# One Strassen chain over all 512 tokens of a block, with the activation sums made by accumulating DMAs

## The chip, the cores and the metric

The kernel runs on one core of a Trainium2 chip. The metric is the device time of one execution in microseconds (us). The kernel before takes 364.61 us (median of three runs, 363.89 to 365.18).

## What is computed

```python
scores = scale * q @ k.T + bias[head, i - j]          # 8 batches, 8 heads, 576 tokens, 64 channels
x = softmax(scores) @ v                               # as 4608 tokens x 512
h = x @ w_in                                          # 512 x 2048
g = h + sin(alpha * h) ** 2 / (alpha + 1e-9)
out = g @ w_out                                       # 2048 x 512
```

## The kernel before, in words

The work is cut in eight **stages**, one for each batch (attention over 576 tokens), and nine **blocks** of 512 tokens for the two products behind it. Stage t does the attention of batch t, then the *input product* of block t: 16 slices f of 128 of the 2048 inner channels, each four matmuls of 512 columns on TensorE (`pb<-xT,w_in`), a sine on ScalarE (L1132), a square on ScalarE or VectorE (L1139, L1141), and on VectorE the sum that gives slice f of `g` (L1146). The *output product* `g @ w_out` of block t runs during the attention of stage t+1, in the places where TensorE would wait for ScalarE. All matmuls are issued by the helper `full` (L500).

In the attention of a stage, runs of three score products (`pb<-qT,kT`) go into three pairs of PSUM banks, ScalarE takes the exponential of each (L749, 128x1024), VectorE multiplies the bias in (L780), TensorE multiplies with the values (`pb<-v,u` and `pb<-vh,u`), VectorE divides (L999, L1000), and the result is turned into `xT` by DMA transposes on SP's queue (L1079, L970) or by TensorE (L1088) with a copy (L581 on ScalarE, L583 on VectorE).

**The output product before.** Of each block's four groups of 128 tokens, two are done plainly (`plan_mo`: 16 matmuls of 512 columns each). The other two are done together by one Strassen-Winograd chain (`plan_chain`): seven products of eight matmuls of 256 columns in place of eight, with combinations of `w_out` made once (`wsum`) and four sums of quarters of `g` made for each block on VectorE (L1364, in four pieces each, into the tile `ss` or in place in `g`). The products are added up on VectorE out of PSUM (`take`, L1421), half a row block at a time, and each 128 tokens are stored (L1409). Blocks 0, 7 and 8 are done otherwise and stay so.

**The order of the work** is set ahead of time by a planner inside the kernel: every piece of work is a task with an estimated duration, dependences and a priority, and `Plan.run` writes the tasks down engine by engine. Each engine then runs its instructions strictly in that order; a wait holds up all that stands behind it on that engine. GpSimd (POOL) and SP issue the DMAs and are such engines too.

**GpSimd's queue before**, in each stage: the copies `kt<-kT` (L445), which wait for the transposed keys of the next batch; a one-element copy (`tick`, L1172) that waits for the first slice of `g`; four loads of values (L450) and two of their tails (L469) for the next batch; and the staging of keys and queries of the batch after that in half precision (L433, DRAM to DRAM).

**SP's queue before**, in each stage: the DMA transposes of `xT`, the stores, and the transposes of the staged keys and queries (L439, L440).

Of the kernel before, what the change touches and what calls it, by code (L numbers as in the profile page):

```python
# [35 lines left out]
NBUF = {"ut": 2, "ss": 1, "u": 2, "g": 2, "s16": 3, "sq": 3, "outs": 5, "xn": 6}  # L36
# [28 lines left out]
class Plan:  # L65


    def __init__(self):
        self.tasks = []
        self.sin = self.in_qk = False  # L70
# [26 lines left out]
    def pick(self, b, taken):  # L97
        sets = PAIRS if b.tag == "sc" else ((6, 7),) if b.tag == "av2" else [(k,) for k in BANKS[b.tag]]
        best = None
# [56 lines left out]
    def run(self, t0):  # L156
        free = {e: t0 for e in ("PE", "ACT", "DVE", "POOL", "SP")}
        todo = list(self.tasks)
        while todo:
            best = None  # L160
            cands = {e: [] for e in free}
# [64 lines left out]
QUOTA = 47  # L226
QUOTA1 = 28
OFFSET = 0
# [20 lines left out]
LATE = 100  # L249
# [8 lines left out]
AV_AT = (3, 4, 6, 7)  # L258
AV_D = (0, 0, 300, 0)
AV_G = (3, 7)  # L260
PRE = -100
# [3 lines left out]
MOEP = (5, 25)  # L265
STEP = 700
MIX = "nnssss"
# [3 lines left out]
MIX0 = "nnssss"  # L271
FIRST = 1
CH = ("mo", "mo", "mo", "st")
PIECES = 4
AV_LATE = 9900
AV0 = 1500
FILL_GAP = 0.05
# [11 lines left out]
AV_PRI = 0  # L289
NORM_PRI = 200  # L290
# [17 lines left out]
def kernel(  # L308
# [78 lines left out]
    xv = zz  # L387
# [13 lines left out]
    def new_g():  # L401
        return tp.tile([128, NF, DM], F16, name="g", tag="g", bufs=2)
# [16 lines left out]
    def new_ss():  # L419
        return tp.tile([128, 6, 512], F16, name="ss", tag="ss", bufs=NBUF["ss"])  # L420

    def new_outs():
        return tp.tile([128, DM], F32, name="outs", tag="outs", bufs=NBUF["outs"])
# [425 lines left out]
    def plan_att(t, gates, gate):  # L849
# [10 lines left out]
        for i, units in enumerate(runs):  # L860
# [20 lines left out]
            def run(e, i=i, made=made, tl=tl, fresh=fresh):  # L881
# [6 lines left out]
                if i == len(runs) - 1:  # L888
                    plan.in_qk = False
# [13 lines left out]
            head = [m]  # L903
            exps += [x[3] for x in made]
# [10 lines left out]
    def plan_late(base, gate):  # L915
# [12 lines left out]
        tail_alone(0, base + 1200)  # L928
        return [x[3] for x in made]

    def tail_alone(t, base):
        tl = plan_tail(t, base)
        m = plan.add({"PE": D_TAIL + 0.1}, tl[0], tl[1], base, new=[tl[2]], use=[tl[3]])
        m.marks = [(tl[4], D_TAIL)]

# [172 lines left out]
    def plan_moe_in(b, tbl):  # L1108
# [5 lines left out]
        for f in range(NF):  # L1114
# [3 lines left out]
            def mm(e, js, f=f, h=h, hb=hb):  # L1118
                if js[0] == 0:
                    h.v = bank(hb)  # L1120
# [22 lines left out]
            def gg(e, f=f, h=h, sq=sq):  # L1143
                if f == 0:
                    gcell[b].v = new_g()
                nc.vector.scalar_tensor_tensor(  # L1146
                    out=gcell[b].v[:, f, :], in0=sq.v, scalar=inv_a[:, f : f + 1], in1=h.v,
# [21 lines left out]
            if f == 0 and 1 <= b < T - 1:  # L1169

                def issue(e):
                    nc.gpsimd.tensor_copy(out=tick, in_=gcell[b].v[0:1, 0, 0:1])  # L1172
                    load_v16(b + 1)

                x = plan.add({"POOL": 6.0}, issue, [gdone[(b, 0)]] + kq_in[-1:], PB + 9500, use=[gbuf[b]])
                staged.append(x)
                if b + 2 < T:
                    to_stage.append((b + 2, x))
# [3 lines left out]
    mo_last, kq_in, staged, to_stage = [], [], [], []  # L1182

    def plan_mo(b, a, cut=NF):

        mb, ob, m = Buf("mo"), Buf("outs"), Cell()
        for f in range(NF):
# [3 lines left out]
            def mm(e, f=f):  # L1191
                if f == 0:
                    m.v = bank(mb)
                full(m.v, gcell[b].v[:, f, 128 * a : 128 * a + 128], w_out16[:, f, :], f == 0, f == NF - 1)
# [43 lines left out]
    def plan_half(b, a):  # L1238
# [10 lines left out]
        def act(i, j):  # L1249
            return gcell[b].v[:, H2 * j : H2 * j + H2, 128 * (a + i) : 128 * (a + i) + 128]  # L1250
# [90 lines left out]
    def plan_chain(b, a):  # L1341

        H2, n = NF // 2, DM // 2
        sv, sb = Cell(), Buf("ss")
        bk = [Buf(x) for x in CH]
        bv = [Cell() for _ in range(4)]
        o = Cell(), Cell()
        ob = Buf("outs"), Buf("outs")
        gall = [gdone[(b, f)] for f in range(NF)]
        base = 500000000 + 4 * b + a  # L1350

        def act(i, j):
            return gcell[b].v[:, H2 * j : H2 * j + H2, 128 * (a + i) : 128 * (a + i) + 128]

        def pre(out, x, y, op, deps, first=False):

            made = []
            for h in range(PIECES):
                r = slice(H2 // PIECES * h, H2 // PIECES * (h + 1))

                def sm(e, h=h, r=r):
# [199 lines left out]
```

## Time and profile before

| | before |
|---|---|
| median of three runs | 364.61 us (363.89 to 365.18) |
| profiled execution, first to last instruction | 361.6 us |
| busy: TensorE / ScalarE / VectorE / GpSimd | 356.0 / 316.3 / 306.1 / 93.2 us |
| granted TensorE clock | 1.000 |
| one stage (187.7 to 226.6 us): length; ScalarE, VectorE busy | 38.9; 36.57, 33.79 us |

The profiled execution has no time of its own beside its span, which is 3.0 us less than the median of the runs. In rows of the profile, `pb<-xT,w_in` reads "written: pb, read: xT and w_in"; `SPq` and `POOLq` are the issuing side of the DMA queues; "x" is a count; durations of merged rows run from the first start to the last end, and matmuls overlap, so the time from one to the next is read from starts.

### The profile page before, as it was taken

What the parts mean: (1) busy time and instruction counts of PE and PEld (TensorE: products, weight loads), DVE (VectorE), ACT (ScalarE), POOL (GpSimd) and SP (SyncE); (2) the same over time, 40 slices, a digit from 0 to 9 for tenths busy, and PEclk for the clock granted to TensorE, in tenths of its full rate; (3) what the DMA queues carried; (4) which work ended last, traced back from release to release, by engine and by line L of the source; (5) the groups of instructions that cost most, each with busy time, mean ns of one, the idle gap of its engine ahead of it and who ended that gap; (6) DMA issues with size and microseconds to landing.
All of it is one profiled execution on the core that took longest, in us unless ns stands there. A gap on an engine that the chain in (4) does not pass through costs nothing.

```text
span 361.6 us, 9613 instructions
## 1 busy us (share of the span) xinstructions
PE 356.0 (98%) x3811; PEld 218.4 (60%) x3811; DVE 306.1 (85%) x749; ACT 316.3 (87%) x436; POOL 93.2 (26%) x135
## 2 busy tenths in 40 slices
PE   8999999999999999999999999999999999999996
PEld 4564445644575447884684458545787467456685
DVE  4887888989977998699978997899869986999982
ACT  2998999999998999899989999899989998996811
POOL 8577450064000820055001900091006000000000
PEclk9999999999999999999999999999999999999999
DMA  9999999789724994299918992699339322001023
GB/s 167 206 200 188 207 160 134 142 83 124 120 48 104 138 150 101 55 158 143 137 34 159 110 169 55 127 136 143 87 81 158 66 57 54 15 3 59 31 76 101
DMA packets 150157, 40.53 MB, mean 112 GB/s; under 512 B 137224, under 2 KB 145504, under 8 KB 150112
## 3 DMA queue, kind: packets, MB, share of 16 engines
q0 software_dynamic: 96064, 17.67, 60.7%
q1 hardware_dynamic: 53872, 22.16, 26.1%
q8 instruction: 30, 0.49, 0.6%
q10 hardware_dynamic: 176, 0.09, 0.1%
q14 instruction: 15, 0.12, 0.1%
HBM read 37.73 MB, written 16.56 MB: 150 GB/s over the span
## 4 chain that ended last, share of the span: by engine, by line
PE 94%; DMA 2%; ACT 1%; DVE 1%; SPq 0%; issue 0%; DVEq 0%
PE pb L500 93%; DMA mhr<-e_dram 1%; ACT u L749 1%; DMA e_dram<-e_sb 1%; PE pb L600 1%; PE pb L1088 1%; DVE u L780 1%; DVE s L1057 0%; SPq L523 0%; ACT e_sb L649 0%; PE pb L594 0%; ACT xT L581 0%; SPq L516 0%; DVE outs L1314 0%; DVE zz L551 0%
## 5 line engine op out<-in xcount | busy, mean ns | idle before, releaser
L749 ACT ACTIVATE u<-pb 128x1024 f16<-128x1024 f32 (+1 forms) x146 | 136.8, 1020 | 6.2 <-PE pb L500 4.9
L500 PE MATMUL pb<-xT,w_in 128*128 128x512 f16 (+4 forms) x704 | 128.6, 340 | 0.3 <-ACT xT L581 0.3
L1146 DVE SCALAR_TENSOR_TENSOR g<-sq,inv_a,pb 128x512 f16<-128x512 f16 x144 | 101.4, 744 | 3.8 <-ACT sq L1139 1.8
L1132 ACT ACTIVATE s<-pb,alphaT 128x512 f16<-128x512 f32 x144 | 92.9, 693 | 12.4 <-PE pb L500 11.6
L500 PEld LDWEIGHTS <-w_in 128*128 128x128 f16 x704 | 64.5, 98 | 56.0 <-issue 0.8
L500 PE MATMUL pb<-w_out,g 128*128 128x512 f16 (+1 forms) x416 | 83.5, 339 | 0.0
L500 PEld LDWEIGHTS <-g 128*128 128x128 f16 x552 | 50.8, 98 | 34.8 <-issue 5.2
L780 DVE TENSOR_TENSOR u<-u,m2r 128x512 f16<-128x512 f16 (+1 forms) x128 | 61.5, 488 | 9.9 <-ACT u L749 9.2
L500 PEld LDWEIGHTS <-u 128*128 128x128 f16 x1280 | 55.9, 97 | 9.6 <-issue 4.9
L1139 ACT ACTIVATE sq<-s 128x512 f16<-128x512 f16 x76 | 47.5, 640 | 2.0 <-DVE g L1146 1.1
L445 POOL COPY kt<-kT 64x256 f16<-64x256 f16 x12 | 5.2, 430 | 168.0 <-DMA kT<-staged_k 167.7
L500 PE MATMUL pb<-v,u 128*128 128x65 f16 x1024 | 43.8, 193 | 0.0
L500 PE MATMUL pb<-qT,kT 64*128 64x64 f16 (+1 forms) x512 | 42.1, 285 | 0.8 <-DVE qT L583 0.3
L1141 DVE TENSOR_TENSOR sq<-s 128x512 f16<-128x512 f16 x68 | 28.4, 427 | 11.3 <-ACT s L1132 10.4
L500 PEld LDWEIGHTS <-kT 64*128 64x128 f16 x512 | 17.2, 94 | 20.5 <-issue 13.1
L500 PE MATMUL pb<-vh,u 128*128 128x130 f16 x128 | 28.3, 221 | 0.2 <-DVE s L1057 0.2
L1000 DVE TENSOR_TENSOR xn<-pb,rd 128x384 f16<-128x384 f32 (+2 forms) x53 | 26.0, 490 | 1.8
L450 POOL DMA_DIRECT2D v<-in_v_dram x28 | 24.7, 895 | 3.1 <-DMA nat<-in_k_dram 1.8
L1459 ACT ACT_TABLE_LOAD x15 | 19.2, 1283 | 0.3
L749 ACT ACTIVATE nat<-pb 128x1024 f16<-128x1024 f32 (+1 forms) x24 | 18.8, 820 | 0.0
L999 DVE RECIPROCAL rd<-pb 128x6 f32<-128x6 f32 (+2 forms) x53 | 9.9, 187 | 8.2 <-PE pb L500 7.0
L500 PE MATMUL pb<-wsum,g 128*128 128x256 f16 (+1 forms) x136 | 16.7, 267 | 0.0
(100 smaller groups left out, 311.7 us busy)
## 6 DMA issues: line engine op xcount, KB each, us to landing
out_dram<-outs SPq DMA_DIRECT2D x28, 256.0 KB, 3.0
v<-in_v_dram POOLq DMA_DIRECT2D x28, 128.0 KB, 4.8
staged_k<-in_k_dram POOLq DMA_DIRECT2D x6, 576.0 KB, 8.6
staged_q<-in_q_dram POOLq DMA_DIRECT2D x6, 576.0 KB, 12.1
w_in<-in_moe_w_in_dram POOLq DMA_DIRECT2D x4, 512.0 KB, 9.1
w_out<-in_moe_w_out_dram POOLq DMA_DIRECT2D x4, 512.0 KB, 13.5
out_dram<-outs SPq DMA_DIRECT2D x16, 128.0 KB, 1.7
w_out<-in_v_dram SPq DMA_DIRECT2D x6, 128.0 KB, 5.1
```

The costliest lines, as they stand in the source:

```text
L445: nc.gpsimd.tensor_copy(out=kts[t % 2][r, :, r], in_=kTs[t % 2][r, :, 512:S])
L450: nc.gpsimd.dma_start(out=vs[t % 2][:, c, :, 0:D], in_=vp[128 * c : 128 * c + 128],)
L500: nc.tensor.matmul(out=out, lhsT=lhsT, rhs=rhs, start=start, stop=stop, skip_group_check=go_on)
L749: nc.scalar.activation(out=o, in_=x, func=AF.Exp, scale=0.125)
L780: nc.vector.tensor_tensor(out=io, in0=io, in1=m2[:, 2 * p : 2 * p + 2, x0 : x0 + hi - lo], op=ALU.mult)
L999: nc.vector.reciprocal(out=r, in_=x[:, :, :, D])
L1000: nc.vector.tensor_tensor(out=xn[:, 0:n].rearrange("p c (z d) -> p c z d", z=2), in0=x[:, :, :, 0:D], in1=r.unsqueeze(3).to_broadcast([128 ...
L1132: nc.scalar.activation(out=s16.v, in_=h.v, func=AF.Sin, scale=alphaT[:, f : f + 1])
L1139: nc.scalar.activation(out=sq.v, in_=s16.v, func=AF.Square)
L1141: k_of(e).tensor_tensor(out=sq.v, in0=s16.v, in1=s16.v, op=ALU.mult)
L1146: nc.vector.scalar_tensor_tensor(out=gcell[b].v[:, f, :], in0=sq.v, scalar=inv_a[:, f : f + 1], in1=h.v, op0=ALU.mult, op1=ALU.add,)
L1459: nc.scalar.preload_act_table_set(name)
```

## The change

Blocks 1 to 6 lose the two plain groups. One chain now does all 512 tokens: seven products of sixteen matmuls of 256 columns. Its sums are no longer made on VectorE. Signs are turned so that only additions are needed, and each sum is a DMA of 512 KB inside SBUF that adds into its target (`accum_op`), issued by GpSimd; two plain copies on SP's queue start two of the sums. `g` is stored in another order, so that each operand of a sum is one run of 4 KB in a partition. The takes are 128x512 in place of 128x256, and a store is 512 KB. The value loads no longer stand behind the first slice of `g`; the planner puts them into the attention of the stage (with `tick` gone from there), and the staging behind the last sum and the value loads. The planner may use any free bank for the output product for a part of the stage (`roomy`), and a dozen of its numbers are others, as `QUOTA` (how much output product goes into the attention), `STEP` and `MOEP`.

```diff
-NBUF = {"ut": 2, "ss": 1, "u": 2, "g": 2, "s16": 3, "sq": 3, "outs": 5, "xn": 6}
+NBUF = {"ut": 2, "ss": 1, "u": 2, "g": 2, "s16": 3, "sq": 3, "outs": 4, "xn": 6}
...
-QUOTA = 47
+QUOTA = 41
...
+V_RUN = 4
+D_ISSUE = 1.0
+D_LAND = 4.5
+D_COPY = 1.1
...
-        return tp.tile([128, NF, DM], F16, name="g", tag="g", bufs=2)
+        return tp.tile([128, 2, 4, NF // 2, 128], F16, name="g", tag="g", bufs=2)
...
                 nc.vector.scalar_tensor_tensor(
-                    out=gcell[b].v[:, f, :], in0=sq.v, scalar=inv_a[:, f : f + 1], in1=h.v,
+                    out=gcell[b].v[:, f // 8, :, f % 8], in0=sq.v.rearrange(four, a=4),
+                    scalar=inv_a[:, f : f + 1], in1=h.v.rearrange(four, a=4),
...
-            if f == 0 and 1 <= b < T - 1:
-
-                def issue(e):
-                    nc.gpsimd.tensor_copy(out=tick, in_=gcell[b].v[0:1, 0, 0:1])
-                    load_v16(b + 1)
...
-    def plan_chain(b, a):
+    def plan_chain(b):
...
+        def act(i, j):
+            return gcell[b].v[:, j, 2 * i : 2 * i + 2]
+
+        def move(to, x, deps, add=True, new=False):
+
+            def go(e):
+                if new:
+                    s2v.v = new_ss()
+                (nc.gpsimd if add else nc.sync).dma_start(
+                    out=to().rearrange("p s f t -> p (s f t)"), in_=x().rearrange("p s f t -> p (s f t)"),
+                    **({"accum_op": ALU.add} if add else {}))
...
+            for f in range(2 * H2):
+
+                def mm(e, f=f):
+                    if f == 0:
+                        bv[k].v = bank(bk[k])
+                    s = f // H2
+                    full(bv[k].v[:, n * s : n * s + n], x()[:, s, f % H2], w()[:, f % H2], f % H2 == 0,
+                         f % H2 == H2 - 1)
...
-        s1 = pre(lambda: sums(0), lambda: act(1, 0), lambda: act(1, 1), ALU.add, gall, True)
-        s2 = pre(lambda: sums(1), lambda: sums(0), lambda: act(0, 0), ALU.subtract, [s1])
-        s3 = pre(lambda: act(1, 0), lambda: act(0, 0), lambda: act(1, 0), ALU.subtract, [s1])
-        s4 = pre(lambda: sums(2), lambda: act(0, 1), lambda: sums(1), ALU.subtract, [s2])
...
+        c2 = move(lambda: sums(0), lambda: act(1, 0), gh[0], False, True)
+        c3 = move(lambda: sums(1), lambda: act(1, 0), gh[0], False)
+        c3.go.after = [c2.go]
+        a2 = move(lambda: sums(0), lambda: act(0, 0), [c2])
+        s3 = move(lambda: sums(1), lambda: act(0, 0), [c3])
+        s2 = move(lambda: sums(0), lambda: act(1, 1), gh[1] + [a2])
+        s1 = move(lambda: act(1, 0), lambda: act(1, 1), gh[1] + [c3, c2])
+        p = prod(0, lambda: act(0, 0), wq(0, 0), gh[0])
+        x = take(0, (1, 0), None, [p], new=True)
+        p = m2 = prod(1, lambda: act(0, 1), wq(1, 0), gh[1])
+        c11 = take(1, (0, 0), (1, 0), [p, x], ALU.add, new=True)
+        s4 = move(lambda: act(0, 1), lambda: sums(0), [s2, m2])
+        p = prod(2, lambda: sums(0), ws(1), [s2] + wdone)
...
+        p = prod(3, lambda: sums(1), ws(2), [s3])
+        p = prod(5, lambda: act(1, 0), ws(0), [s1])
+        p = prod(4, lambda: act(1, 1), ws(3), [])
+        p = prod(6, lambda: act(0, 1), wq(1, 1), [s4])
...
+            if t < T - 1:
+                x = plan.add({"POOL": 5.0}, lambda e, t=t: load_v16(t + 1), [heads[V_RUN]] + heads[len(RUNS.split()):],
+                             PB + 9300)
```

`gh[0]` and `gh[1]` are the first and the last eight slices of `g`; a sum waits for its copies and sums by name, so **s2 waits for a2, which waits for the copy c2**.

**GpSimd, from one batch's `kt` copies to the next one's**, before:

```order
L445 COPY kt_70<-kT_66 64x4x64 x2
L1172 COPY tick<-g 1x1
L450 DMA v_72<-in_v_dram 128x8x64 x4
L469 DMA vh_74<-in_v_dram 64x4x64 x2
L433 DMA staged_k<-in_k_dram 4608x1x64
L433 DMA staged_q<-in_q_dram 4608x1x64
L445 COPY kt_71<-kT_67 64x4x64 x2
```

and now, where `ss<-g` and `g<-g` and `g<-ss` are the five adding DMAs a2, s3, s1, s2 and s4:

```order
L455 COPY kt_70<-kT_66 64x4x64 x2
L1366 DMA ss<-g 128x2048 x2
L1366 DMA g<-g 128x2048
L1366 DMA ss<-g 128x2048
L1366 DMA g<-ss 128x2048
L460 DMA v_73<-in_v_dram 128x8x64 x4
L479 DMA vh_75<-in_v_dram 64x4x64 x2
L443 DMA staged_k<-in_k_dram 4608x1x64
L443 DMA staged_q<-in_q_dram 4608x1x64
L455 COPY kt_71<-kT_67 64x4x64 x2
```

The value loads and the staging moved behind all five sums of the block; before, they were the first thing behind the `kt` copies.

**TensorE in block 3, at the first product that reads a sum.** Before (third product of the chain, in the later attention):

```order
L500 MATMUL pb<-v_72,u 128x65
L500 LDWEIGHTS ss
L500 MATMUL pb<-wsum,ss 128x256 [waits DVE_49]
L500 LDWEIGHTS ss
L500 MATMUL pb<-wsum,ss 128x256
```

and now (product 2, whose weights are sum s2):

```order
L510 MATMUL pb<-w_out_79,g 128x256
L510 LDWEIGHTS g
L510 MATMUL pb<-w_out_79,g 128x256
L510 LDWEIGHTS ss [waits DMASW1_49]
L510 MATMUL pb<-wsum,ss 128x256 [waits DVE_49]
L510 LDWEIGHTS ss
L510 MATMUL pb<-wsum,ss 128x256
```

The wait for VectorE's sums became a wait for a DMA of GpSimd's queue, and it stands directly behind product 1, with nothing between that could cover it.

**VectorE behind the input product of a block**, before:

```order
L1364 TENSOR_TENSOR ss<-g 128x256 x4
L999 RECIPROCAL rd<-pb 128x4
L1000 TENSOR_TENSOR xn<-pb,rd 128x256
L780 TENSOR_TENSOR u<-u,m2r 128x2x256
L780 TENSOR_TENSOR u<-u,m2r 128x2x384
L583 COPY outs<-pb 128x512
L780 TENSOR_TENSOR u<-u,m2r 128x2x384
L1364 TENSOR_TENSOR ss<-ss,g 128x256
L766 TENSOR_TENSOR u<-u,mhr 128x2x128
L1364 TENSOR_TENSOR ss<-ss,g 128x256
```

and now:

```order
L1422 TENSOR_TENSOR outs<-pb,outs 128x2x256
L790 TENSOR_TENSOR u<-u,m2r 128x2x256
L1011 RECIPROCAL rd<-pb 128x4
L1012 TENSOR_TENSOR xn<-pb,rd 128x256
L790 TENSOR_TENSOR u<-u,m2r 128x2x384
L593 COPY outs<-pb 128x2x256
L790 TENSOR_TENSOR u<-u,m2r 128x2x384
L776 TENSOR_TENSOR u<-u,mhr 128x2x128
```

The sums are gone from between the bias products, and the takes that stay are twice as wide.

More of the change, by code (lines that the diff above doesn't have):

```diff
@@ L98, in pick @@
         sets = PAIRS if b.tag == "sc" else ((6, 7),) if b.tag == "av2" else [(k,) for k in BANKS[b.tag]]
+        if b.tag == "mo" and self.roomy:
+            if all(self.bank_free(k) is None or self.bank_free(k) > self.now for k in (6, 7)):
+                sets = [(k,) for k in range(8)]
         best = None
@@ L160, in run @@
             best = None
+            self.now = free["PE"]
             cands = {e: [] for e in free}
@@ L1405, in ws, with put, take @@
             return lambda: wsum[:, k]
-        def store(i):
-            r = 512 * b + 128 * (a + i)
-            nc.sync.dma_start(out=out[r : r + 128, :], in_=o[i].v)
-        def take(k, to, x, deps, new=False, last=False):
+        def put(i, j):
+            return o[i].v[:, :, n * j : n * j + n]
+        def take(k, to, x, deps, op=None, swap=False, new=False, last=False):
             i, j = to
```

176 lines of the change are left out of this document (77 added, 99 removed).

## Prediction

> **What bounds the kernel now.** I read the page first, then the chain that ended last, then one stage by windows.
>
> ```profile
> PE 356.0 (98%) x3811; PEld 218.4 (60%) x3811; DVE 306.1 (85%) x749; ACT 316.3 (87%) x436; POOL 93.2 (26%) x135
> ...
> PE 94%; DMA 2%; ACT 1%; DVE 1%; SPq 0%; issue 0%; DVEq 0%
> ```
>
> TensorE is busy 356.0 of 361.6 us and is 94% of the chain. The chain in order of time shows how its stages follow each other (start, length):
>
> ```profile
> 148.83 38.83 PE pb L500 x468
> 187.66 0.17 PE pb L1088 x3
> 187.83 38.73 PE pb L500 x403
> 226.55 0.17 PE pb L1088 x3
> ```
>
> No other engine stands between stages of 38.9 us. But a busy TensorE may wait inside its rows, so I set ScalarE beside it in one stage's windows: input product, turn to the attention, attention.
>
> ```profile
> 188.60:202.40 13.80, 13.80 (x66) 6.26 (x64) 12.07 (x24) 12.30 (x21) 5.04 (x8) 1.00 0.79 126
> 202.40:205.00 2.60, 2.60 (x15) 1.10 (x15) 2.60 (x5) 2.58 (x5) 2.60 (x3) 1.00 2.16 146
> 205.00:227.50 22.50, 22.50 (x333) 15.41 (x333) 19.12 (x59) 21.69 (x24) 2.83 (x2) 1.00 1.10 109
> ```
>
> The columns are length, then TensorE, weight loads, VectorE, ScalarE and GpSimd busy, granted clock, DMA share and GB/s. In the 22.5 us of attention ScalarE is busy 21.69, VectorE 19.12. So TensorE bounds the stage, with ScalarE 0.8 us behind it; VectorE has 3 us to spare. What is taken from TensorE counts until ScalarE has closed up.
>
> **What the change takes from TensorE.** The times of one matmul are read from starts in the timeline.
>
> ```profile
> 188.59 13.98 PE L500 MATMUL pb<-xT,w_in 128*128 128x512 f16 x64
> 202.40 0.27 PE L500 MATMUL pb<-w_out,ss 128*128 128x256 f16 x1
> ...
> 204.98 0.82 PE L500 MATMUL pb<-qT,kT 64*128 64x512 f16 x6
> 205.73 0.25 PE L500 MATMUL pb<-vh,nat 128*64 128x130 f16 x2
> ...
> 347.93 2.78 PE L500 MATMUL pb<-wsum,u 128*128 128x256 f16 x24
> 350.55 1.04 PE L500 MATMUL pb<-w_out,u 128*128 128x256 f16 x8
> ```
>
> 64 matmuls of 512 columns take 202.40 - 188.59 = 13.81 us, 0.2158 each; 24 of 256 take 2.62, 0.1092 each. A block's output product was 32 x 0.2158 + 56 x 0.1092 = 13.02 us and becomes 112 x 0.1092 = 12.23: **0.79 us less, 4.7 us in six blocks**.
>
> Where it goes matters. Between input product and first score run stood 1 matmul of 256 and 11 of 512 columns (23 halves), now 28 halves: 0.5 us more there; the attention has 13 halves, 1.4 us, less. ScalarE is busy 21.69 us in that attention, of which one copy into `xT` (0.49 us, first row) goes to VectorE in these stages. The other rows are its waits in this one stage, in all, how often, the longest:
>
> ```profile
> 226.84 0.49 ACT L581 ACTIVATE xT<-pb 128x384 f16<-128x384 f16 x1
> ...
> ACT s L1132 <- PE pb L500: 1.5, 2, 1.2
> ACT u L749 <- PE pb L500: 0.4, 2, 0.2
> ```
>
> With 21.2 of work and the waits of 0.2 us still before a score run, the attention can't be shorter than some 21.4 us. Then the stage is 13.8 + 3.15 + 21.4 = 38.35, 0.55 us less than now, and by TensorE alone 0.79. **I take 0.6 us a block, 3.6 in all**: at such a balance the second engine keeps part, and both ends stay in the range.
>
> **VectorE.** The sums go and the takes grow:
>
> ```profile
> L1421 DVE TENSOR_TENSOR outs<-pb,outs 128x256 f32<-128x256 f32 x30 | 12.6, 420 | 1.4 <-PE pb L500 1.2
> L583 DVE COPY outs<-pb 128x512 f32<-128x512 f32 x16 | 11.0, 689 | 0.6 <-PE pb L500 0.3
> L1364 DVE TENSOR_TENSOR ss<-ss,g 128x256 f16<-128x256 f16 x24 | 6.9, 287 | 0.0
> ```
>
> Sixteen pieces of 0.29 us are 4.6 us a block; seven takes and copies of 0.42 and two copies of 0.69 were 4.3 and become eight of 0.69, 5.5. VectorE loses 3.4 us a block, none of it on the path, since TensorE hides it: I cost it at nothing. A take can now hold a bias product back 0.27 us longer; three score pairs in flight cover that, without them it is 0.27 us for each.
>
> **The new wait.** Call the start of an input product M (188.59 here). TensorE reaches product 2 in block 3 after the input product (13.8), 55 halves (6.0), two score runs and the tail of the attention before (0.75 each, from the starts 204.98 and 205.73), and one pair of 512 columns (0.43): M + 22.5. What must have landed by then is c2, a2, s2, one after the other. The slices of `g` on VectorE set their start:
>
> ```profile
> 198.08 2.05 DVE L1146 SCALAR_TENSOR_TENSOR g<-sq,inv_a,pb 128x512 f16<-128x512 f16 x3
> ...
> 203.21 2.10 DVE L1146 SCALAR_TENSOR_TENSOR g<-sq,inv_a,pb 128x512 f16<-128x512 f16 x3
> ```
>
> The first row holds slices 7 to 9 (counted from 0), the second ends with 15: eight slices are there at M + 10.2, all at M + 16.7. No trace row shows an adding DMA, nor one of 512 KB inside SBUF. The nearest is a store of 256 KB in whole rows, in a window of 0.0725 us columns:
>
> ```profile
> GB/s 0 0 0 0 0 0 0 0 0 0 0 0 282 367 424 424 395 367 282 424 367 226 57 0 18 95 201 219 201 124 42 4 0 0 1 0 0 0 0 0
> ...
> out_dram<-outs SPq DMA_DIRECT2D x1, 256.0 KB, 2.0
> ```
>
> It lands 2.0 us after its issue and moves for 0.7 us, near 380 GB/s. A copy of 512 KB is then 2.7 us. GpSimd takes longer to issue than SP (shortest, median and longest in ns):
>
> ```profile
> L450 POOL DMA_DIRECT2D v<-in_v_dram x28: 873/893/907, 33.4 to 276.9; - x28
> ...
> L1409 SPq DMA_DIRECT2D out_dram<-outs x12: 336/337/338, 110.9 to 325.5; - x12
> ```
>
> For a sum I put the lower end at 3.3 (a copy and those 0.55 us), and the upper end, for one alone, at 4.6 (every byte moved twice); below a copy it can't be, since it moves the same bytes. I take 3.9, between them. c2 lands at M + 13.0, a2 at 17.0, s2 is issued behind s1 at 17.7 and lands at 21.6: **0.9 us before it is needed, cost nothing**. That cover is thin, and each further us of a sum counts twice.
>
> **What moved on GpSimd and SP.** The value loads and the staging, before and in the rows of the page:
>
> ```profile
> 198.60 3.54 POOL L450 DMA_DIRECT2D v<-in_v_dram  x4
> 202.10 1.29 POOL L469 DMA_DIRECT2D vh<-in_v_dram  x2
> 203.34 2.28 POOL L433 DMA_DIRECT2D staged_k<-in_k_dram  x1
> 205.04 2.80 POOL L433 DMA_DIRECT2D staged_q<-in_q_dram  x1
> ...
> 229.56 2.57 SPq L439 DMA_TRANSPOSE kT<-staged_k  x1
> 232.22 2.68 SPq L440 DMA_TRANSPOSE qT<-staged_q  x1
> ...
> staged_q<-in_q_dram POOLq DMA_DIRECT2D x6, 576.0 KB, 12.1
> ```
>
> Staged queries land at 205.04 + 12.1 = 217.1 and are fetched at 232.22: 15 us of slack. Now they stand behind s4, which needs product 1 (M + 22.5): values from 23.4, queries issued at 29.8 (6.4 us on, as 198.60 to 205.04), landed at M + 41.9, against a fetch 4.7 us into the next input product, 38.3 + 4.7 = 43.0. **1.1 us of slack is left of 15**: it costs nothing while s4 is on time. Behind the waiting transpose on SP stand c2 and c3, due 5.5 us later, so only a delay of over 3 us goes round into the next block's sums. The `xT` transposes of the attention now meet the staging. The tail's pair (207 to 210 us, first row) already does, and lands in 6.6 us where the median of all `xT` transposes (second row) is 2.8:
>
> ```profile
> DMA to landing us min/median/max: 6.4/6.6/6.7
> ...
> DMA to landing us min/median/max: 2.3/2.8/6.7
> ```
>
> Between the value products whose transpose is needed last and the next input product stand, in the new order, 29 halves (3.2 us), one score run of 0.83 and five value products of 0.30:
>
> ```profile
> 222.24 0.90 PE L500 MATMUL pb<-qT,kT 64*128 64x512 f16 x34
> 223.07 1.27 PE L500 MATMUL pb<-wsum,g 128*128 128x256 f16 x10
> ...
> 224.39 0.22 PE L500 MATMUL pb<-vh,u 128*128 128x130 f16 x1
> ...
> 224.69 0.22 PE L500 MATMUL pb<-vh,u 128*128 128x130 f16 x1
> ```
>
> That is 5.5 us, less 0.8 for the division on VectorE: cost nothing at 2.8, at 6.6 up to 1.9 us a block; I keep nothing, since that pair is the slowest shown. Four output buffers for five: the previous block's last store is issued near M + 17, lands by 20, is needed at 22.5. No cost.
>
> **Sum.** 361.6 - 3.6 = 358.0 for the span; with the 3.0 us between span and median of the runs, **361.0 us**.
>
> **Rivals.**
> *TensorE alone sets the stage*: all 4.7 us, perhaps a little more where ScalarE waited: 357.5 to 359.3. For it: ScalarE has 0.8 us; against it: all of that would have to vanish.
> *ScalarE holds most of it, or small waits at product 2*: 362.6 to 365. For it: 21.69 of 22.5.
> *The sums come late (the slower side).* Place: product 2, with the next score runs and so ScalarE behind it. a2, s3, s1 and s2 share GpSimd's queue. If each byte is moved twice, each needs 4 x 0.65 = 2.6 us of all engines; four from M + 13.9 end at 24.3, and s2 lands at about 25.0, 2.5 us late. Less the 0.79 gained that is 1.7 us a block, 10 in all: 375. It decides from a landing at M + 23.3. For it: a sum has two sources; against it: four overlap only if s1, which waits for all of `g`, falls in with s2.
> *The staging comes late*: s4 over 3 us late sends the delay round, 1 us a block and more, 365 to 370.
> *GpSimd is held up by VectorE.* The value loads stand beside a VectorE 87% busy (12.07 of 13.80 us), and their issues are 873 to 907 ns each. One that waited out an L1146 instruction (some 0.7 us, three in 2.05) would spread them; a2 and s2 each that late are 1.5 us, 0.6 past the cover. The kernel would then stand at 361.0 + 3.6 = 364.6, and I give it 0.02. The Trainium skill, "SBUF — State Buffer", section "SBUF: two separate sides", says that a VectorE instruction in a two-port mode locks GpSimd out so that it can't write the descriptors of its DMAs. By that rule this is the rival that bites; the trace disagrees so far, at 873 to 907 ns.
>
> The skill's "DMA: Bandwidth & Descriptors", section "Anatomy of one DMA", puts a DMA at about 2.0 us plus its bytes at 436 GB/s. An estimate from that page for 256 KB is 2.6 us, where the store row has 2.0; for a sum of 512 KB with each byte twice it is 4.4, and s2 would land at M + 22.6, the sum unchanged to 0.1 us.
>
> **Chances.** Forecast (359.3 to 362.6) 0.48; TensorE alone 0.10; ScalarE or small waits 0.14; sums late 0.21; staging late 0.05; GpSimd held 0.02. A measurement of this kernel tells about 0.3% from no change, 1.1 us. Faster: 0.48 + 0.10 + 0.04 of the third = 0.62. Within 0.3% (363.5 to 365.7): 0.10 of the third, the 0.02, and 0.01 of the late cases, 0.13. Slower: 0.25. For 8 in 10 the range leaves out 0.05 below 358.5 and 0.13 of the late cases above 368.
>
> **What would show it.** Right: stages near 38.3 us, no wait of TensorE for a DMA of `ss`, sums landing in 3.3 to 4.6 us, ScalarE's waits below 0.2 us in the attention. Sums late: a gap of TensorE before product 2 or score rows spread there, landings over 5 us. Staging late: SP's transposes of `qT` later than 5 us into the input product. ScalarE: no gap, but exponentials end to end. Wrong altogether would be a stage of 38.9 with none of these.

## The result, and the profile after

The changed kernel takes 429.06 us (median of 4 runs, 422.76 to 429.58) against 364.62 us (363.89 to 365.18). The ratio is **1.168, 95% interval 1.159 to 1.177**: slower by a sixth, where 361.0 us was forecast and 368.0 was the range's end. Two of the four runs, 429.19 and 429.58 us, count as slow ones, so the ratio is that of the other two, 422.76 and 428.94 us. The profiled run took 428.94 us, with a span of 426.9 us and a mean granted clock of 0.943.

The page after, in the order in which it was read before: busy time of the engines; the largest group of matmuls that waits now and did not before; queue 0 (software, 60.7% before); and the issues with their median landing.

```profile
PE 367.2 (86%) x3955; PEld 236.2 (55%) x3955; DVE 295.9 (69%) x649; ACT 311.6 (73%) x428; POOL 118.3 (28%) x159
...
q0 software_dynamic: 100384, 33.40, 81.0%
...
L510 PE MATMUL pb<-wsum,ss 128*128 128x256 f16 x192 | 31.1, 314 | 42.6 <-DMA ss<-g 42.6
...
ss<-g POOLq DMA_DIRECT2D x18, 512.0 KB, 6.9
ss<-g SPq DMA_DIRECT2D x12, 512.0 KB, 3.6
out_dram<-outs SPq DMA_DIRECT2D x12, 512.0 KB, 7.2
...
g<-g POOLq DMA_DIRECT2D x6, 512.0 KB, 10.6
```

TensorE was busy 356.0 of 361.6 us, idle for 5.6. It is now busy 367.2 of 426.9, idle for 59.7. So the 65.3 us of span are 54.1 us of idle time and 11.2 us of longer busy time. Of the idle time 42.6 us are waits for DMAs into `ss`, where products 2 and 3 read their sums. The waits, in all, how often, and the longest (the first row is from the kernel before):

```profile
ACT u L749 <- PE pb L500: 4.9, 17, 1.0
...
ACT u L759 <- PE pb L510: 61.8, 27, 9.4
...
PE pb L510 <- DMA ss<-g: 42.6, 6, 8.3
...
DVE outs L1422 <- DMA out_dram<-outs: 18.4, 5, 5.7
```

Six waits, one in each block, 7.1 us each. The score runs that stand behind product 2 on TensorE start after it, and ScalarE waits with them (61.8 us, 4.9 before). One stage by windows shows it; input product, turn, attention, columns as before.

```profile
166.86:182.37 15.51, 14.13 (x130) 11.53 (x128) 12.43 (x25) 12.33 (x21) 1.59 (x3) 1.00 1.18 181
182.37:185.53 3.16, 3.16 (x31) 2.64 (x29) 3.16 (x6) 3.14 (x5) 0.99 (x2) 1.00 0.89 165
185.53:217.14 31.61, 23.89 (x340) 17.09 (x340) 16.17 (x40) 20.47 (x23) 11.83 (x11) 0.84 1.46 158
```

The input product has 1.4 us of waits for `xT`, the turn is as forecast, and the attention takes 31.6 us in place of 22.5. In that attention the timeline (start, length, engine, what; idle time before it in brackets) has GpSimd's adds first, then SP's issues, then TensorE:

```profile
181.57 0.91 POOL L1366 DMA_DIRECT2D ss<-g  x1 [6.12 <-DVE g L1161]
182.88 0.87 POOL L1366 DMA_DIRECT2D ss<-g  x1 [0.40 <-issue]
185.68 0.84 POOL L1366 DMA_DIRECT2D g<-g  x1 [1.93 <-DVE g L1161]
186.76 0.85 POOL L1366 DMA_DIRECT2D ss<-g  x1 [0.23 <-issue]
199.19 0.85 POOL L1366 DMA_DIRECT2D g<-ss  x1 [11.59 <-issue]
...
178.06 1.13 SPq L1366 DMA_DIRECT2D ss<-g  x2
184.10 2.29 SPq L1425 DMA_DIRECT2D out_dram<-outs  x2
188.04 6.17 SPq L982 DMA_TRANSPOSE xT<-xn  x2
...
190.13 1.37 PE L510 MATMUL pb<-w_out,g 128*128 128x256 f16 x11
198.72 1.67 PE L510 MATMUL pb<-wsum,ss 128*128 128x256 f16 x7 [7.21 <-DMA ss<-g]
```

The adds are a2, s3, s1, s2 and s4, from above. M is 166.86. a2 is issued at M + 14.7. s1 waits for the last slices of `g` on VectorE (L1161) and goes out at M + 18.8. s2 follows right behind it at M + 19.9, by when a2 has landed, 5.1 us after its issue. TensorE is ready for product 2 at M + 24.6. It starts at M + 31.9, so s2 landed some 11.9 us after its issue. Ahead of it in GpSimd's queue are s3 and s1. Beside it on the same 16 DMA engines are two stores of 512 KB and two transposes. The transposes are late too: all into `xT` land in 7.4 us (median), where it was 2.8.

```profile
DMA to landing us min/median/max: 2.3/7.4/11.4
```

The longer busy time is seen behind the gaps, in matmuls at a lower clock. In the rows below the same eight value products take 0.41 us ahead of the gap and 0.65 behind it. The granted clock (third figure from the end of a window's row) is 0.50 for the seven matmuls that TensorE runs at the end of the window with the gap, 0.65 from 200 to 206 us, and 1.00 again from 206 to 212. In the run no_sums below, which has no wait for sums, as many matmuls are busy for 353.9 us in place of 367.2.

```profile
164.13 0.41 PE L510 MATMUL pb<-v,u 128*128 128x65 f16 x8
...
201.81 0.65 PE L510 MATMUL pb<-v,u 128*128 128x65 f16 x8
...
194.00:200.00 6.00, 1.28 (x7) 0.88 (x7) 1.49 (x3) 0.00 (x0) 0.81 (x2) 0.50 0.51 93
200.00:206.00 6.00, 6.00 (x61) 3.53 (x60) 2.66 (x6) 3.58 (x4) 6.00 (x8) 0.65 1.34 137
206.00:212.00 6.00, 5.88 (x112) 4.42 (x109) 4.53 (x13) 5.84 (x8) 3.33 (x2) 1.00 2.48 141
```

### The profile page after: what moved, and what is told of

The parts are those of the page before. It is cut to its first block, busy times and chain, and to the rows that moved or that the text cites. A ratio compares the mean times of both kernels' runs of the same rounds, so it can differ in the third digit from the quotient of the medians.

```text
span 426.9 us, 9833 instructions
## 1 busy us (share of the span) xinstructions
PE 367.2 (86%) x3955; PEld 236.2 (55%) x3955; DVE 295.9 (69%) x649; ACT 311.6 (73%) x428; POOL 118.3 (28%) x159
## 5 line engine op out<-in xcount | busy, mean ns | idle before, releaser
L759 ACT ACTIVATE u<-pb 128x1024 f16<-128x1024 f32 (+1 forms) x146 | 135.9, 1023 | 62.0 <-PE pb L510 61.8
L510 PE MATMUL pb<-xT,w_in 128*128 128x512 f16 (+4 forms) x704 | 130.8, 343 | 5.9 <-DMA xT<-xn 5.6
L1161 DVE SCALAR_TENSOR_TENSOR g<-sq,inv_a,pb 128x512 f16<-128x512 f16 x144 | 101.4, 743 | 3.9 <-ACT sq L1153 2.6
L510 PEld LDWEIGHTS <-g 128*128 128x128 f16 x648 | 60.4, 98 | 17.1 <-issue 2.5
L510 PE MATMUL pb<-wsum,ss 128*128 128x256 f16 x192 | 31.1, 314 | 42.6 <-DMA ss<-g 42.6
L510 PE MATMUL pb<-w_out,g 128*128 128x256 f16 (+1 forms) x416 | 59.7, 289 | 0.2 <-DVE xn L1012 0.2
L510 PE MATMUL pb<-qT,kT 64*128 64x64 f16 (+1 forms) x512 | 47.3, 300 | 4.2 <-ACT u L759 3.5
L510 PEld LDWEIGHTS <-ss 128*128 128x128 f16 x192 | 19.5, 111 | 48.3 <-DMA ss<-g 44.3
L510 PE MATMUL pb<-v,u 128*128 128x65 f16 x1024 | 45.3, 197 | 0.0
L1422 DVE TENSOR_TENSOR outs<-pb,outs 128x512 f32<-128x512 f32 x30 | 20.5, 684 | 18.4 <-DMA out_dram<-outs 18.4
L510 PEld LDWEIGHTS <-kT 64*128 64x128 f16 x512 | 16.7, 96 | 25.7 <-issue 19.9
L1366 POOL DMA_DIRECT2D ss<-g x18 | 15.9, 881 | 49.5 <-DVE g L1161 28.4
L510 PE MATMUL pb<-wsum,g 128*128 128x256 f16 (+1 forms) x232 | 29.1, 269 | 0.0
```

What stands on the lines that cost most here:

```text
L510: nc.tensor.matmul(out=out, lhsT=lhsT, rhs=rhs, start=start, stop=stop, skip_group_check=go_on)
L759: nc.scalar.activation(out=o, in_=x, func=AF.Exp, scale=0.125)
L1161: nc.vector.scalar_tensor_tensor(out=gcell[b].v[:, f // 8, :, f % 8], in0=sq.v.rearrange(four, a=4), scalar=inv_a[:, f : f + 1], in1=h.v.r ...
L1366: (nc.gpsimd if add else nc.sync).dma_start(out=to().rearrange("p s f t -> p (s f t)"), in_=x().rearrange("p s f t -> p (s f t)"), **({"ac ...
L1422: nc.vector.tensor_tensor(out=put(i, j), in0=m, in1=put(*x), op=op)
```

## The experiments

Three theories stood at first. **One**: an adding DMA is slow in itself, and the four of a block stand in each other's way. **Two**: the adds are as fast as copies, and other traffic (stores, transposes, the moved loads and staging) delays them. **Three**: GpSimd is held up by VectorE as it issues them. A time without an interval is a single run; runs of the changed kernel itself lie between 422.8 and 429.6 us, so a few us between single runs mean nothing. All times together (waits of TensorE for DMAs into `ss` and into `xT`, and median landing of the transposes into `xT`, from the profiled run of each):

| kernel | us | ratio to before (95%) | wait for ss | wait for xT | xT landing |
|---|---|---|---|---|---|
| before | 364.6 | | | 0 | 2.8 |
| after | 429.1 | 1.168 (1.159 to 1.177) | 42.6 | 5.6 | 7.4 |
| plain_moves | 386.2 | | 10.4 | 4.2 | 5.6 |
| s2_first | 406.4 | | 10.8 | 12.7 | 8.6 |
| small_stores | 414.0 | | 28.5 | 4.7 | 6.8 |
| land_12 | 445.9 | | 0 | 34.8 | 7.3 |
| sums_dve | 381.1 | 1.046 (1.044 to 1.049) | | 0.7 | 4.9 |
| dve_small_stores | 374.7 | 1.028 (1.025 to 1.032) | | 0 | 5.0 |
| no_sums | 368.6 | 1.010 (1.006 to 1.014) | | 0 | 3.4 |
| no_sums_small_stores | 366.0 | 1.004 (1.002 to 1.006) | | 0.4 | 3.0 |
| before_values_moved | 364.6 | 1.000 (0.998 to 1.003) | | 0 | 3.6 |
| after_values_back | 444.9 | | 46.3 | 1.1 | 5.8 |
| dve_values_back | 383.9 | 1.053 (1.049 to 1.057) | | 0 | 2.3 |
| two_and_two | 384.5 | 1.056 (1.049 to 1.062) | 0 | 11.2 | 6.5 |
| two_values_back | 371.4 | 1.020 (1.015 to 1.026) | 0 | 3.1 | 5.0 |
| two_stage_early | 383.8 | 1.051 (1.045 to 1.057) | 0 | 0.7 | 3.9 |
| one_stage_early | 382.9 | 1.051 (1.047 to 1.055) | 0 | 0 | 3.0 |

**adds_alone.** A kernel of its own, of which this is the core; `bar` makes the next group wait for all before it.

```diff
+    def add(to, x):
+        nc.gpsimd.dma_start(out=to, in_=x, accum_op=ALU.add)
...
+    for _ in range(4):
+        add(three, src)
+    bar()
...
+    for _ in range(2):
+        add(one, src)
+        add(two, src)
+        add(three, src)
+        add(four, src)
+        bar()
```

> The adding DMAs by themselves, with no product, no attention and no other traffic unless it is named: in turn, each after the one before has landed, 512 KB copies issued by SyncE, 512 KB copies issued by GpSimd, 512 KB adds, 256 KB adds, 128 KB adds and 512 KB adds of float32; then two copies at once, two adds at once, four adds at once; then one add beside two 512 KB stores, beside one staging of 576 KB, beside six transposing DMAs, and beside VectorE additions. (The kernel leaves out the reference's computation and stores a constant.) Theory 1, an add is slow in itself and the four stand in each other's way: one add alone lands 5 to 7 us after its issue, against 3 to 3.5 us for a copy, two at once have the second land 4 us later, four at once land their last at 14 to 18 us; float32 lands sooner or later by how the price goes with elements or bytes. Theory 2, other traffic: one add alone lands within 4 us, four at once within 8, and only beside the stores, the staging or the transposes does one reach 7 to 12 us. Theory 3, GpSimd is held up by VectorE while it issues: only the add beside VectorE's additions lands late, by 2 us or more.

The DMA issues by window (count, KB each, median us to landing): four copies in two pairs; four adds in turn; 256 KB; 128 KB; four adds at once (`one` stands for two, since the next group's first falls into the window); one of three beside two stores (the other two landed in 6.2 and 5.1 us); one beside VectorE at work.

```profile
one<-src POOLq DMA_DIRECT2D x2, 512.0 KB, 2.9
two<-src POOLq DMA_DIRECT2D x2, 512.0 KB, 3.7
...
three<-src POOLq DMA_DIRECT2D x4, 512.0 KB, 4.5
...
four<-src POOLq DMA_DIRECT2D x4, 256.0 KB, 3.3
four<-src POOLq DMA_DIRECT2D x4, 128.0 KB, 2.6
...
one<-src POOLq DMA_DIRECT2D x2, 512.0 KB, 4.8
two<-src POOLq DMA_DIRECT2D x1, 512.0 KB, 6.8
three<-src POOLq DMA_DIRECT2D x1, 512.0 KB, 8.8
four<-src POOLq DMA_DIRECT2D x1, 512.0 KB, 10.8
...
three<-src POOLq DMA_DIRECT2D x1, 512.0 KB, 6.0
...
one<-src POOLq DMA_DIRECT2D x1, 512.0 KB, 4.5
```

The engines' share in two windows: four adds in turn, and four copies in two pairs (length, VectorE and GpSimd busy, clock, DMA share, GB/s).

```profile
35.48:54.43 18.95, 0.02 (x1) 3.39 (x4) 1.00 0.58 111
104.75:114.02 9.27, 0.83 (x13) 2.11 (x4) 1.00 0.57 226
```

An add alone lands in 4.5 us, 1.6 more than a copy. It takes 18.95 x 0.58 / 4 = **2.75 us of all 16 engines, a copy 9.27 x 0.57 / 4 = 1.32**. The next one in line lands 2.5 us later (2.0 between the landings, which count from issues 0.53 us apart), so the fourth of four lands 10.8 us after its issue. Theory one has the kind right, and its sizes were too large (5 to 7 us alone, 14 to 18 for four). Theory two, 4 us alone and 8 for four, is out as the whole cause, though two stores beside it make 5.1 to 6.2 us of 4.5, one staging 4.9 to 6.3 and six transposes 4.6 to 6.2 (three trials each, some with the group before still under way). Adds of 512 KB of float32 were issued 4.8 us apart, each when the one before had landed, as those of float16. Nothing speaks for theory three: beside VectorE's additions, the one instruction of VectorE tried here, an add lands in the same 4.5 us, and the 30 adds of the changed kernel take 0.84 to 1.08 us to issue.

**plain_moves.**

```diff
-                    **({"accum_op": ALU.add} if add else {}))
+                    )
```

> The changed kernel with the addition taken out of its 30 adding DMAs, which become plain copies of the same 512 KB, issued by the same engine in the same places with the same waits; every other instruction stands where it stood. (The sums of the activations are left out: the destination is overwritten.) Theory 1, the addition itself is what is slow: the copies land in about 3.5 us, TensorE's wait for ss, 42.6 us now, falls under 6 us, the software queue's share from 81% to 55 to 62%, and the time to 362 to 372 us. Theory 2, queue and neighbours: a copy of as many bytes in the same place is as late, the wait stays over 25 us and the time over 405 us. Theory 3, GpSimd held up while it issues: as theory 2.

386.2 us. The addition alone, with every instruction in its place, is some 43 us of the 64 (one run against the median). But neither range is met. What is left over the kernel before is 21.5 us, with 10.4 of waits for `ss`: even a copy into `ss` lands up to 8.1 us after its issue in that crowd.

**s2_first.**

```diff
+        s3.go.after, s1.go.after = [s2.go], [s3.go]
```

> The changed kernel with the order of the adds on GpSimd changed: the second of the chain that product 2 waits for (s2) is issued ahead of those of product 3 (s3) and product 5 (s1) instead of behind them. Theory 1, the adds share a rate (about 4 us of all the DMA engines for each): product 2 starts some 4 to 5 us earlier in each block, but products 3 and 5 now wait for s3 and s1, which land as late as s2 did, so that the waits move from product 2 to 3 and 5 and the time stays within 1.5% of the changed kernel's, 423 to 435 us. Theory 2, an add is fast once it is at the head of the queue: s2 lands 4 to 5 us after its issue, the wait of 7 us for product 2 goes for the most part, nothing new comes, and the time is 385 to 400 us.

406.4 us, between the two. The wait for `ss` falls from 42.6 to 10.8 us, but TensorE now waits 12.7 us for `xT` (5.6 in the changed kernel), whose transposes land in 8.6 us. So the order on the queue is worth 23 us and doesn't mend it.

**small_stores.**

```diff
-                        out=out[r : r + 256].rearrange("(s p) n -> p s n", s=2), in_=o[i].v)
+                        out=out[r : r + 256, 0:64].rearrange("(s p) n -> p s n", s=2), in_=o[i].v[:, :, 0:64])
```

> The changed kernel with the output stores of blocks 1 to 6 cut to 64 of 512 columns, an eighth of the bytes (seven eighths of these rows of the output are left out). Theory 1, the adds stand in each other's way: an add beside two 512 KB stores landed 0.5 to 1.7 us later than one alone, so product 2 comes 1 to 2 us earlier in a block and the time is 412 to 424 us. Theory 2, the stores are what delays them, or VectorE's 28 us of waiting for stores is what the time is made of: under 405 us.

414.0 us, as theory one had it. The wait for `ss` is 28.5 us, 14 less, 2.3 a block: the stores that stand beside s2 account for that much of its landing.

**land_12.**

```diff
-D_LAND = 4.5
+D_LAND = 12.0
...
-                         [], PB + 9000, after=tbl + [
+                         [], PB + 9000, after=tbl + [stg[x] for x in (t + 1,) if x in stg] + [
```

> The changed kernel with one number of the planner changed, the time that an add takes to land: 12 us in place of 4.5 (and the next-but-one block's staging named as a condition of its loads, which changes no order by itself). The same instructions in another order. If the loss is only that the plan was made with a landing time that is too short, the wait for ss (42.6 us) falls by more than half and the time to 385 to 405 us. If the chain of two adds is longer than the work that can stand before product 2 (the plan has only the output product's first 44 matmuls and the first scores), the wait moves about and the time stays over 410 us.

445.9 us: the plan with the longer time has no wait for `ss` left and is slower still. TensorE waits for transposes (34.8 us) and for staged queries (15.7 us) instead. So this longer guess of the landing time does not save the change, since the transfers are still there to be made; values between 4.5 and 12 us were not tried.

**sums_dve and dve_small_stores.**

```diff
-        a2 = move(lambda: sums(0), lambda: act(0, 0), [c2])
-        s3 = move(lambda: sums(1), lambda: act(0, 0), [c3])
-        s2 = move(lambda: sums(0), lambda: act(1, 1), gh[1] + [a2])
-        s1 = move(lambda: act(1, 0), lambda: act(1, 1), gh[1] + [c3, c2])
+        s3 = pre(lambda: sums(1), lambda: act(1, 0), lambda: act(0, 0), gh[0], True)
+        s2 = pre(lambda: sums(0), lambda: sums(1), lambda: act(1, 1), gh[1] + [s3])
+        s1 = pre(lambda: act(1, 0), lambda: act(1, 0), lambda: act(1, 1), gh[1] + [s3])
```

> The changed kernel with the sums made by VectorE (four additions of 128x2048 elements a block in four pieces each, each sum in the tile where the DMAs had put it) and without the moves; the chain over 512 tokens, the value loads and the staging stay as changed. Theories 1 and 2 alike: TensorE's wait for ss goes, the time falls to 360 to 370 us; VectorE gets some 4.5 us more in a block, which its bias products may pass on to ScalarE and TensorE (up to 375 us). If the chain over 512 tokens, the four buffers of outs or the moved staging cost something of their own, the time stays over 380 us, with VectorE's wait for the stores (28 us in the changed kernel) as large as it was.

> The kernel with the sums by VectorE (381.1 us) with the output stores of blocks 1 to 6 cut to an eighth of the bytes in the same way. If its 16.5 us over the kernel before come from the four buffers of outs, which are free again only when a 512 KB store has landed: 364 to 371 us. If they come from VectorE's load (323 us busy against 306 before, 37 us in a stage of 40): 376 to 382 us.

381.1 us: this is the time expected if something beside the adds costs (over 380), but VectorE waits 6.4 us for stores and not the 28 us that were expected with it. Without any adding DMA the change is still 16.5 us slower. VectorE has more to do than in the kernel before (323.3 against 306.1 us), four sums of four pieces at 0.42 us:

```profile
PE 357.0 (94%) x3955; PEld 231.7 (61%) x3955; DVE 323.3 (85%) x744; ACT 310.6 (82%) x429; POOL 92.2 (24%) x129
```

With small stores it is 374.7 us, between the two ranges. So 6.4 of the 16.5 us are the stores, and 10 stay.

**no_sums and no_sums_small_stores.** These tell the sums from the rest, and test all other steps of the forecast at once.

```diff
-        p = prod(2, lambda: sums(0), ws(1), [s2] + wdone)
+        p = prod(2, lambda: act(1, 0), ws(1), gh[1] + wdone)
...
-        p = prod(3, lambda: sums(1), ws(2), [s3])
+        p = prod(3, lambda: act(1, 1), ws(2), [])
```

> The changed kernel without the sums of the activations and without their moves: products 2, 3, 5 and 6 read the quarters of the activations as they are (the sums are left out), everything else of the change stays: one chain for 512 tokens, its takes, four buffers, 512 KB stores, value loads in the attention. If all other steps of the forecast hold (0.6 us a block of TensorE saved, takes, stores, loads and staging hidden): 359 to 363 us. If the chain's takes and stores cost what sums_dve and plain_moves still lose: 370 to 382 us, with waits of VectorE for stores and of TensorE for takes.

> The kernel without the sums (368.6 us) with the output stores of blocks 1 to 6 cut to 64 of 512 columns, an eighth of the bytes (seven eighths of these rows of the output are left out). If the stores and the four buffers hold the 7.6 us that are missing from the forecast: 361 to 364 us, and VectorE's wait for stores (8.5 us) under 3. If TensorE's saving isn't there, or ScalarE and the transposes keep it: 366 to 370 us.

368.6 us, between the two ranges: slower than before by 1.0% even with no sums. Made by VectorE, the sums are 12.5 us more. In no_sums VectorE waits 8.5 us for stores at its copies (L593). The smaller stores take all but 0.9 of that wait and 2.6 us of time away, and 366.0 us is still not the 361 to 364 of the forecast. TensorE's page row and its largest wait in no_sums_small_stores:

```profile
PE 352.9 (97%) x3955; PEld 230.7 (63%) x3955; DVE 295.2 (81%) x649; ACT 310.7 (85%) x428; POOL 91.2 (25%) x129
...
PE pb L510 <- ACT u L759: 4.2, 9, 0.5
```

TensorE is 3.1 us less busy than before, but idle for 11.2 of 364.1 us (before 5.6). It waits nine times, up to 0.5 us, for ScalarE's exponentials, where the kernel before has one such wait of 0.3 us.

**before_values_moved, after_values_back, dve_values_back.** One part alone, and the same part undone.

```diff
-                x = plan.add({"POOL": 6.0}, issue, [gdone[(b, 0)]] + kq_in[-1:], PB + 9500, use=[gbuf[b]])
...
+                x = plan.add({"POOL": 5.0}, lambda e, t=t: load_v16(t + 1), [heads[4]] + heads[len(RUNS.split()):],
+                             PB + 9300)
```

> The kernel before with one part of the change alone: its value loads moved from the input product into the attention of the same block, as the change has them; sums by VectorE, chain over 256 tokens, five buffers as before. If the move is harmless, as the forecast had it: 363 to 367 us. If it makes staging or transposes late by itself: 369 to 380 us.

> The changed kernel with one part undone: the value loads are issued where the kernel before had them, on GpSimd behind the first column of the activations, ahead of the block's adds and not behind its last one. If the adds themselves are all of the loss, nothing moves but by the half copy of the queue: 420 to 435 us. If the loads and the staging behind them, which now run in the next attention beside its transposes and adds, are a part of it: 395 to 418 us, with v landing under 7 us and shorter waits for xT.

> The kernel with the sums by VectorE (381.1 us) and the value loads put back in the same way, so that of the change only the chain over 512 tokens, its takes, stores and buffers are left. If the moved loads and the staging that follows them cost something without any add: 368 to 376 us. If not: 378 to 384 us, and what is over the kernel before comes from VectorE's load and the stores alone.

The move alone changes nothing: 1.000 (0.998 to 1.003). Undone where VectorE makes the sums it gains nothing (383.9 us). Undone in the changed kernel it makes 444.9 us, which neither side expected: the six loads now stand on GpSimd's queue right ahead of a2.

```profile
233.14 3.54 POOL L460 DMA_DIRECT2D v<-in_v_dram  x4
236.63 1.30 POOL L479 DMA_DIRECT2D vh<-in_v_dram  x2
238.54 0.90 POOL L1375 DMA_DIRECT2D ss<-g  x1 [0.60 <-DVE g L1161]
...
248.47 0.83 POOL L1375 DMA_DIRECT2D ss<-g  x1 [5.31 <-DMA ss<-g]
```

From a2 to s2, which waits for a2's landing, it is 9.9 us here, 5.2 in the changed kernel. The planner's order around it changed too, so only the sign of this run is used.

**two_and_two, two_values_back, two_stage_early, one_stage_early.** Search for a version that keeps some adds: the early sums on VectorE, and of the late ones (s1, s4) both or one by DMA, with loads and staging in other places.

```diff
-        s1 = pre(lambda: act(1, 0), lambda: act(1, 0), lambda: act(1, 1), gh[1] + [s3])
+        s1 = move(lambda: act(1, 0), lambda: act(1, 1), gh[1] + [s3])
...
-        s4 = pre(lambda: act(0, 1), lambda: act(0, 1), lambda: sums(0), [s2, m2])
+        s4 = move(lambda: act(0, 1), lambda: sums(0), [s2, m2])
```

> The changed kernel with the sums divided: the two that stand in ss and are needed first (s3 and s2) by VectorE, in four pieces each, the two that are needed last (s1 in place in the activations, s4) by adding DMAs; no copies by SyncE. Theory A, what costs is adds that are waited for: two adds a block with 8 us or more before their product cost nothing, VectorE carries 3.4 us a block less than where it made all four sums, and the time is 360 to 370 us. Theory B, the adding DMAs cost wherever they stand, since they hold the engines that the transposes and the staging need: 375 to 395 us, with waits for xT or for s1 and s4 in TensorE's list.

> The kernel with two sums by VectorE and two by adding DMAs (384.5 us) and the value loads put back. If what it loses (11.2 us of TensorE's waits for xT) comes from staging that starts behind s4 and six value loads and so falls on the transposes at the attention's end: 366 to 377 us and xT's wait under 4 us. If two adds a block cost as much by themselves: 380 to 387 us.

> The kernel with two sums by VectorE, two by adding DMAs and the value loads put back (371.4 us), with the staging issued right behind the value loads, ahead of the block's two adds, no longer behind the last of them, so that it runs in the input product. If the staging on the queue behind s4 is what still makes transposes late (3.1 us of waits for xT): 361 to 368 us. If the staging now falls on the block's first transposes and the adds: 372 to 385 us.

> The same with one adding DMA a block (s4, the last needed) and three sums by VectorE, which gets 1.7 us more in a block. If each add costs where it stands: 2 to 4 us faster than with two. If VectorE's load is what counts (323 us busy with four sums at 381 us, 308 with two at 371): 3 to 6 us slower than with two.

Two adds that nobody waits for don't make the kernel fast either: two_and_two takes 384.5 us with no wait for `ss`, and TensorE waits 11.2 us for `xT` instead. Loads ahead of the two adds make 371.4 us, the best of the four. Staging ahead of them as well makes 383.8: the adds land in 11.3 and 7.4 us there, against 5.2 and 5.3 without, and VectorE waits 14.9 us for stores (10.1 of them at its takes), TensorE 7.9 us for the takes behind them.

```profile
g<-g POOLq DMA_DIRECT2D x6, 512.0 KB, 11.3
g<-ss POOLq DMA_DIRECT2D x6, 512.0 KB, 7.4
```

One add less, with 1.7 us a block more for VectorE, changes nothing there (382.9 us), so that the two prices could not be told apart by it. No version was faster than the kernel before.

**What is settled.** Theory one, with a part of two: each add takes 2.75 us of all engines, four are issued within 5.2 us, and the stores, transposes, loads and staging of the same stretch share the engines with them, so that whichever of them stands first makes the others late. Step by step from the kernel before: +4.0 us for all but the sums (no_sums), +17.5 for moves of the same bytes (plain_moves), +42.9 for the addition. Only the last step keeps every instruction in its place; for the other two the planner made a new order, and plain_moves is a single run, so how much is due to the moves and how much to the rest is rough. What holds the last 10 us of sums_dve and the last 5 of no_sums_small_stores (366.0 against the 361.0 forecast) was not taken further apart.

## Why the prediction was wrong

- **What bounds the kernel**: right for the kernel before; after the change it is a wait.
- **TensorE's saving of 3.6 us**: the work is less (busy 352.9 to 353.9 us without sums, 356.0 before), but 2 to 3 us and not 4.7, and the time doesn't fall even with the sums left out. That is the rival "ScalarE holds most of it, or small waits" (362.6 to 365) and a little over it.
- **VectorE loses 3.4 us a block**: 306.1 to 295.9 us is 1.7. The pieces' durations overlap, so that their sum overstated it: in the kernel before, a piece of 0.29 us starts 0.20 us after the one before it. VectorE also makes ten copies into `xT` where it made four. Off the path, as forecast.
- **The new wait: the step that failed**, in the term "s2 is issued behind s1 at 17.7 and lands at 21.6". The price of one add was nearly right: taken at 3.9 us between 3.3 and 4.6 "for one alone", measured 4.5 alone. Wrong was to price s2 like an add alone, as if s3 and s1 ahead of it in the same queue took nothing. Measured are 11.9 us from issue to landing. The issue was 2.2 us late as well, at M + 19.9: s1, which stands ahead of it, got the last slices of `g` at M + 18.8 and not 16.7, and a2, issued 1.6 us late, took 5.1 us beside s3 where 3.9 was assumed.
- **The rival "the sums come late"** had the mechanism, the place and the engine time (2.6 us each; 2.75 measured), with a chance of 0.21. Its price was too small, 2.5 us late and 375 in all. It laid the four adds alone from M + 13.9 to 24.3, but product 2 started at M + 31.9. Two stores in the same stretch account for 2.3 us a block (small_stores); the transposes there share the engines too, their part was not measured by itself. Nor did it count what follows from a gap: matmuls at a lower clock, and transposes that land late.
- **Values and staging moved, cost nothing**: right by itself (1.000). Wrong together with the adds: the median of the kernel before (2.8 us for a transpose) was kept for a stretch that the change fills with adds and staging, and it became 7.4. With two adds, loads put ahead of them take 384.5 us to 371.4; with all five, the same move made it worse (444.9).
- **Four buffers of `outs`, no cost**: wrong. VectorE waits 18.4 us at L1422 and 10.0 at L593 for stores after the change, and not at all before. The 512 KB stores land in 7.2 us. The row that was used, 2.0 us for 256 KB, was one store; the median of the 28 on the page was 3.0. How much the four buffers cost by themselves was not tried. The stores' bytes are worth 15 us in the changed kernel (one run), 6.4 in sums_dve and 2.6 in no_sums.
- **GpSimd held by VectorE**, given 0.02: not seen. The 18 issues of adds into `ss` take 0.84 to 1.00 us, and beside VectorE at work adds_alone shows 0.84 and a landing of 4.5. VectorE's additions were the only instruction tried by itself. No run here shows the lock that the Trainium skill states in "SBUF — State Buffer", section "SBUF: two separate sides".
- The estimate from the Trainium skill, "DMA: Bandwidth & Descriptors", section "Anatomy of one DMA", of 4.4 us for an add that moves each byte twice agrees with the 4.5 us of one alone. The section is about DMAs that GpSimd issues, so the store row that the prediction set beside it, which SP issued, was no test of it. The estimate is a price for a transfer that has the engines to itself, and 11.9 us is what four and their neighbours made of it.

## What to carry to other kernels

Price a DMA twice: by its landing when alone, and by the time that it takes of all engines, summed over everything that is issued in the same stretch; whoever waits for the last of them pays the second. Where several transfers precede a waited-for one in a queue, lay them one behind the other before looking at the cover, and add the stores and transposes that are already there. Work moved from a busy engine to the DMAs isn't off the path if small transposes that feed the next stage share those DMAs.

## What was not expected of the hardware

- A DMA of 512 KB within SBUF that adds takes 2.75 us of all 16 engines, 2.1 times a copy's 1.32, and lands in 4.5 us alone; each further one queued lands 2.5 us later. One of 256 KB alone lands in 3.3 us, one of 128 KB in 2.6. GpSimd takes 0.84 us to issue it, 0.53 for a copy.
- Behind the gap of 7.2 us TensorE ran on at a lower granted clock: 0.50 for the first seven matmuls, 0.65 over the 6 us from 200 on, and 1.00 only in the 6 us after that. Eight value products took 0.65 us in place of 0.41.
